# Joining chunk 0's inverse halves on TensorE, and moving raw-word transfers to SyncE's queue

## The chip, the cores and the metric

The kernel runs on one core of one Trainium2 chip. The time is device microseconds of one execution, as the median over several executions. A core has TensorE (PE, matrix multiply), VectorE (DVE), ScalarE (ACT), GpSimd (POOL) and SyncE (SP), each with its own instruction queue that runs in order; the queues wait for each other through semaphores. DMAs are issued here from SyncE's and GpSimd's queues. TensorE's clock is granted by a throttle, and the profile shows how much of full speed it was given.

## The reference

Two stages. A delta-rule recurrence over 768 steps for 4 batches and 8 heads, head dimension 48, and a feed-forward block on its output. Cut to what matters:

```python
k_n = k / (np.linalg.norm(k, axis=-1, keepdims=True) + 1e-06)
for t in range(S):                       # S = 768, state is (B, H, 48, 48)
    y[:, :, t] = einsum('bhd,bhde->bhe', q[:, :, t], state)
    v_old = einsum('bhde,bhd->bhe', state, k_n[:, :, t])
    state += beta[:, :, t, None, None] * outer(k_n[:, :, t], v[:, :, t] - v_old)
x = y.transpose(0, 2, 1, 3).reshape(3072, 384)
h = x @ w_in                             # (384, 2048)
out = (h / (1 + exp(-1.702 * h))) @ w_out  # (2048, 384)
```

The arithmetic is float32. The weights `moe_w_in` and `moe_w_out` arrive as 64-bit words; the kernel fetches them raw and turns them into float32 on VectorE.

## The kernel before, in words

The sequence is cut into 6 chunks of 128 steps. A *unit* is one chunk of one batch (8 heads), so there are 24 units; chunk 0 holds units 0 to 3. Inside a chunk the recurrence becomes a triangular solve: with G the Gram matrix of the normalized keys, the corrected values U satisfy (I + tril(beta G)) U = V. The 128 rows are cut into four blocks of 32 (`BS`). For each of the 128 diagonal blocks of a chunk (4 batches, 8 heads, 4 blocks: one per SBUF partition) VectorE builds the 32x32 inverse; the rest is block substitution on TensorE.

**The inverse** (`invert`, line 440) works on two tiles, `NT` (the blocks, row by row in the free dimension) and `YB` (their inverse, starting as the identity, stored with columns j before rows i). Sub-blocks of 8 are inverted row by row, pairs of 8 are joined to 16 (the `QS < HS` part), and the two halves of 16 are joined to 32: the lower left quarter is minus Y1 N10 Y0. Every product is a VectorE multiply into a scratch tile `P` followed by a reduce (`dots`). For chunk 0 the result is then transposed block by block into `YT` on the partitions of the time steps, and multiplied per unit by a scale (`zs[:, 5]`, beta over the squared norm) into `XB`, kept in `inverse[b]`.

**The hops** (`hops`, line 994, and `together`). A unit's solve is four times: U of block `blk` = XB times V (`solve`, psU, 8 matmuls of 32x32 on 48 columns), copied from PSUM by ScalarE (`solved`), then G times U for the blocks below (`below`, psR), subtracted from V by VectorE (`rest`). Two units alternate, so that eight hops (the loop at line 1033) solve units 0 and 1, and eight more units 2 and 3. Between hops the loop lays other work by hand: `ahead_of(preparing, 1)` (the keys of chunk 1: ScalarE squares, a VectorE sum, GpSimd's power, a VectorE scaling, then transposes, Gram matrices `G` and their way through DRAM into `NT`), `fill(n)` (n VectorE steps of the conversion of raw weight words), the scaling of V of units 2 and 3 (`values_scaled`, ScalarE), the causal masking of score tiles (`select`, GpSimd) and `warm(n)` (n throw-away bf16 matmuls of 128x256 on TensorE). After the hops `put_out` forms the outputs psY and the state; the first feed-forward matmuls (`ph`) follow.

**In front of the hops** TensorE transposes the keys (psT), forms the diagonal blocks (`diagonal`, psD) that VectorE scales into `D_` and turns into `NT`, the Gram matrices of chunk 0 (`gram`, psG, copied to G by ScalarE) and the scores of all four units (`scores`: psT of q, ScalarE's copy to QS, psQ, four ScalarE copies to M). PSUM is in three pools: `ps_big` (2 banks), `ps_moe` (2) and `ps_seq` (4). Chunk 0's psG uses `ps_moe` throughout, psT `ps_big`, psQ one pair in `ps_big` and one in `ps_seq`.

**The order** is that of the program: most instructions around the change are pinned (`Engine`, `pinned`; the helper is line 102, so the profile shows them all as L102). VectorE, ScalarE and GpSimd run them in that order, as does each DMA queue.

**Raw words.** `w_in` is fetched in four quarters by `fetch_in` (line 172). A quarter is three parts `j` of 128 rows, a part four DMAs: 48 and 16 rows for each half of the partitions. Quarters 0, 1 and 3 land in `w_out`'s tile (3 in the place of 0), quarter 2 in three spare tiles `homes` ("raw"). In quarters 0 to 2 the half for partitions from 64 on is issued by GpSimd's queue (`other_queue`), the other by SyncE's. A conversion step on VectorE waits for the words it reads. Each queue keeps eight DMAs under way: one more waits for the one eight places ahead.

## Time and profile before

| | |
|---|---|
| median of 3 executions | 773.48 us (773.38 to 776.35) |
| the profiled execution | 771.55 us, span 769.8 us |
| mean granted TensorE clock | 0.977 of full |
| TensorE busy | 743.6 us, 97% of the span |
| TensorE weight loads | 558.0 us, 72% |
| VectorE busy | 439.8 us, 57% |
| ScalarE busy | 240.1 us, 31% |
| GpSimd busy | 128.4 us, 17% |

The page gives busy time per engine over the whole span and in 40 slices of 19.2 us, each a digit in tenths. A busy TensorE counts the throw-away matmuls too. A timeline line reads: start, duration, engine, line, operation, output<-inputs, partitions x elements, count, and in brackets the idle time before it with what ended it. A float32 matmul appears as two records, so psU's 8 matmuls are x16. A table of stretches gives for each its length, then the busy time of PE, PEld, DVE, ACT and POOL with the number of instructions, the granted clock, the DMA engines' share and GB/s.

### The profile page before, as it was taken

The page shows a single profiled execution, that of the slowest core. Times are in us where ns is not written, and L with a number is a line of the kernel's source. Part 1 is how long each engine was busy: PE and PEld are TensorE (multiplying, and loading weights), DVE is VectorE, ACT ScalarE, POOL GpSimd, SP SyncE. Part 2 cuts the span into 40 slices and gives each one's busy share as a digit, 9 for nine tenths or more (in the row PEclk, how much of TensorE's full clock was granted, in tenths as well). Part 3 has the DMA queues.
Part 4 walks back from the last instruction along what each step waited for, and adds up shares of the span by engine and source line. Part 5 has one row for each costly group of instructions (what it writes and reads, how often), then busy time and mean ns, then how long its engine had stood idle before and what let it go on. Part 6 is the DMA issues. An engine that isn't in the chain of part 4 may idle for free.

```text
span 769.8 us, 19471 instructions
## 1 busy us (share of the span) xinstructions
PE 743.6 (97%) x8508; PEld 558.0 (72%) x8508; DVE 439.8 (57%) x896; ACT 240.1 (31%) x535; POOL 128.4 (17%) x133
## 2 busy tenths in 40 slices
PE   7888999888999999999999999999999999999997
PEld 6666788556687687687688678678678677686774
DVE  5999897996766566566566566565566521000000
ACT  4567523343233233133133133124123132121110
POOL 6133301100222122122131121220210000000000
PEclk8599999989999999999999999999999999999999
DMA  9965355543142142142142142142030020000000
GB/s 158 173 121 114 86 146 124 141 107 82 40 96 57 37 93 56 37 95 56 35 96 57 34 97 56 25 107 57 22 81 9 24 42 2 17 11 1 26 1 21
DMA packets 131637, 50.78 MB, mean 66 GB/s; under 512 B 106432, under 2 KB 127040, under 8 KB 131552
## 3 DMA queue, kind: packets, MB, share of 16 engines
q1 hardware_dynamic: 129152, 41.27, 24.9%
q0 software_dynamic: 2400, 8.26, 4.4%
q8 instruction: 67, 1.10, 0.6%
q14 instruction: 18, 0.15, 0.1%
HBM read 32.08 MB, written 16.25 MB: 63 GB/s over the span
## 4 chain that ended last, share of the span: by engine, by line
PE 83%; DVE 8%; SPq 4%; issue 1%; ACT 1%; DMA 1%; POOL 0%; DVEq 0%; ACTq 0%
PE ph L102 32%; PE po L102 30%; PE psY L102 6%; PE psU L102 5%; SPq L102 4%; PE psQ L102 3%; PE psR L102 3%; PE psG L102 2%; DVE w_out L102 2%; PE psT L102 2%; DVE tmp L102 2%; DVE P L102 1%; DVE V L102 1%; DVE w_in L102 1%; DMA w_out<-in_moe_w_in_dram 1%
## 5 line engine op out<-in xcount | busy, mean ns | idle before, releaser
L102 PE MATMUL po<-w_out,gT 128*128 128x384 f32 x768 | 263.4, 494 | 3.3 <-DVE w_out L102 3.3
L102 PE MATMUL ph<-xT,w_in 128*128 128x256 f32 x1152 | 261.2, 383 | 0.3
L102 PEld LDWEIGHTS ph<-xT,w_in 128*128 128x128 f32 x1152 | 214.8, 190 | 32.5 <-issue 1.7
L102 PEld LDWEIGHTS po<-w_out,gT 128*128 128x128 f32 x768 | 142.2, 191 | 96.3 <-DVE w_out L102 4.2
L102 DVE TENSOR_TENSOR V<-V,psR 128x384 f32<-128x384 f32 (+2 forms) x72 | 40.1, 557 | 191.6 <-PE psR L102 191.0
L102 ACT ACTIVATE gT<-ph 128x512 f32<-128x512 f32 x96 | 56.5, 596 | 150.8 <-PE ph L102 150.7
L102 DVE TENSOR_TENSOR P<-NT,YB 64x8 f32<-64x8 f32 (+26 forms) x178 | 85.2, 479 | 4.7
L102 ACT COPY US<-psU 32x384 f32<-32x384 f32 x92 | 43.2, 470 | 139.6 <-PE psR L102 75.5
L102 PEld LDWEIGHTS psU<-V,XB 32*32 32x32 f32 x1536 | 58.3, 104 | 35.8 <-issue 25.6
L102 DVE TENSOR_REDUCE YB<-P 64x4 f32<-64x8 f32 (+27 forms) x178 | 77.2, 434 | 6.3 <-DVE P L102 0.2
L102 PE MATMUL psU<-V,XB 32*32 32x48 f32 x1536 | 69.5, 203 | 4.0 <-DVE V L102 3.9
L102 PE MATMUL psR<-US,G 32*32 32x48 f32 x2576 | 62.9, 204 | 1.0 <-issue 0.5
L624 POOL TENSOR_SCALAR_AFFINE_SELECT M<-M 128x1024 f32<-128x1024 f32 x20 | 25.1, 1253 | 220.9 <-DVE M L102 160.1
L102 PEld LDWEIGHTS psR<-US,G 32*32 32x32 f32 x2576 | 53.4, 104 | 2.0 <-issue 1.0
L102 PE MATMUL psQ<-QS,kT 48*128 48x176 f32 (+1 forms) x384 | 39.1, 350 | 5.4 <-ACT QS L102 5.4
L102 PEld LDWEIGHTS psQ<-QS,kT 48*128 48x128 f32 x384 | 32.1, 215 | 9.0 <-ACT QS L102 7.2
L102 DVE TENSOR_TENSOR P<-NT 64x256 f32<-64x256 f32 (+7 forms) x44 | 36.3, 825 | 0.3
L102 DVE TENSOR_REDUCE NT<-P 64x64 f32<-64x1024 f32 (+7 forms) x44 | 35.4, 803 | 1.5
L102 PE MATMUL psG<-kT 48*128 48x128 f32 x384 | 32.1, 304 | 1.9 <-ACT G L102 1.2
L102 ACT COPY o<-po 128x384 f32<-128x384 f32 x24 | 11.5, 479 | 71.5 <-issue 41.0
L87 POOL DMA_DIRECT2D KN<-in_k_dram x13 | 12.4, 953 | 116.1 <-PE psY L102 107.0
L102 ACT COPY M<-psQ 128x256 f32<-128x256 f32 x68 | 22.9, 377 | 24.8 <-DVE V L102 17.5
(102 smaller groups left out, 609.7 us busy)
## 6 DMA issues: line engine op xcount, KB each, us to landing
Nd<-G SPq DMA_DIRECT2D x16, 512.0 KB, 3.5
QP<-in_q_dram SPq DMA_DIRECT2D x24, 192.0 KB, 3.9
V<-in_v_dram SPq DMA_DIRECT2D x24, 192.0 KB, 3.3
out_dram<-o SPq DMA_DIRECT2D x24, 192.0 KB, 2.0
KN<-in_k_dram POOLq DMA_DIRECT2D x14, 192.0 KB, 3.8
NT<-Nd SPq DMA_DIRECT2D x20, 128.0 KB, 2.6
Yd<-YS SPq DMA_DIRECT2D x20, 128.0 KB, 2.5
XB<-Yd SPq DMA_DIRECT2D x20, 128.0 KB, 3.0
```

What stands on the lines that cost most here:

```text
L87: dma(out=dst[n % len(dst)][:, :, 0:D], in_=src[b, :, c * C : (c + 1) * C, :].rearrange("h p d -> p h d"),)
L102: return lambda *a, **kw: tc.keep_in_program_order(op(*a, **kw))
L624: (pool if self.n < B else nc.gpsimd).affine_select(out=self.M, in_=self.M, compare_op=ALU.is_gt, fill=0.0, base=0, pattern=[[0, H], [1, 1 ...
```

## The change

Chunk 0's inverse stops at the halves of 16. VectorE transposes the upper half's columns of Y into `YT`, the lower half into `Yb` (in `NT`, its other columns zeroed by GpSimd) and the lower columns into `YT`. `joined` then joins the halves of one unit on TensorE in two steps, one yield each: psZ (32 matmuls from `D_`, the 32x32 blocks, and Y1 transposed), copied over `D_` by ScalarE, and psC (32 matmuls with Yb), which VectorE subtracts from `YT` before it forms XB. Unit 0 is joined before the hops, unit 1's psC follows the first hop's solve, and units 2 and 3 are joined in hops 1 to 4. `YT` lies in the third spare tile of quarter 2.

Around it: psG of units 1 and 3 uses `ps_big`; the scores of units 0 to 2 are formed two transposes ahead with bursts of 4 warm matmuls between, those of unit 3 in hops 2 and 3; the burst before the joins is 12 in place of 26 in front of the hops (`NY`), and in the first eight hops 5 in each but hop 3, which has none, where it was 11 in the first three and 5 in the others. GpSimd's queue keeps its half of quarter 0; quarters 1 and 2 are issued by SyncE alone, the last part of each after the joins that free its place. q of unit 3, k of unit 6 and 7 (`seventh`), the values of units 2 and 3, q of unit 4 and the later betas change places in SyncE's queue.

```diff
-    NW, NY, NU = 14, 26, 11
+    NW, NS_, NY, NU = 14, 4, 12, 11
-    def fetch_in(i, other=None):
+    def fetch_in(i, other=None, js=range(KC)):
-        for j in range(KC):
+        for j in js:
 def gram(n):
-        pool_, tag = (ps_moe, "moe") if c == 0 else (ps_big, "big")
+        pool_, tag = (ps_moe, "moe") if c == 0 and b % 2 == 0 else (ps_big, "big")
 def invert(c, b0=0, nb=B):
+        if c == 0:
+            by_d = Yb.rearrange("p d j -> p j d")
+            vec.transpose(YT.rearrange("p d i -> p i d")[:, HS:], Y.rearrange("p j i -> p i j")[:, HS:])
+            pool.memset(Yb[:, :, HS:], 0.0)
+            vec.transpose(by_d[:, 0:HS], Y[:, 0:HS])
+            vec.transpose(YT.rearrange("p d i -> p i d")[:, 0:HS], Y.rearrange("p j i -> p i j")[:, 0:HS])
+            yield 0.0
+            return
-        if c == 0:
-            T = wk.tile([128, BS, BS], F32, tag="P", name="YT")
-            vec.transpose(T.rearrange("p d i -> p i d"), Y.rearrange("p j i -> p i j"))
-            for b in range(B):
-                XB = wk.tile([128, H, BS], F32, tag="XB", name="XB", bufs=4)
-                tt(XB, T[:, b * H : (b + 1) * H], zs[:, 5, b].broadcast_to([128, H, BS]), op=ALU.mult)
-                inverse[b] = XB
-                yield 0.0
-            return
+    def joined(bs):
+        HS, n = BS // 2, len(bs)
+        d = slice(bs[0] * H, (bs[-1] + 1) * H)
+        blocks = [slice(blk * BS, (blk + 1) * BS) for blk in range(NB)]
+        Z = D_[:, bs[0] : bs[-1] + 1, :, 0:HS]
+        ps = ps_moe.tile([128, n, H, HS], F32, tag="moe", name="psZ")
+        for i, b in enumerate(bs):
+            for h in range(H):
+                for r in blocks:
+                    pe.matmul(ps[r, i, h, :], lhsT=D_[r, b, h, :], rhs=YT[r, b * H + h, HS:], start=True, stop=True)
+        act.copy(Z, ps)
+        yield
+        ps = ps_moe.tile([128, n, H, HS], F32, tag="moe", name="psC")
+        for i, b in enumerate(bs):
+            for h in range(H):
+                for r in blocks:
+                    u = slice(r.start, r.start + HS)
+                    pe.matmul(ps[r, i, h, :], lhsT=Yb[u, b * H + h, :], rhs=Z[u, i, h, :], start=True, stop=True)
+        vec.tensor_tensor(YT[:, d, HS:], YT[:, d, HS:], ps.rearrange("p n h i -> p (n h) i"), op=ALU.subtract)
+        for b in bs:
+            XB = wk.tile([128, H, BS], F32, tag="XB", name="XB", bufs=4)
+            vec.tensor_tensor(XB, YT[:, b * H : (b + 1) * H], zs[:, 5, b].broadcast_to([128, H, BS]), op=ALU.mult)
+            inverse[b] = XB
+        yield
 # the loads in front
-    for b in range(B):
+    for b in range(B - 1):
         load(b, ((QP, q),), sync)
-    for n in range(B, len(KN)):
+    for n in range(B, len(KN) - 1):
         load(n, ((KN, k),), sync)
-    fetch_in(1, other_queue)
-    for b in range(HB, B):
-        load_values(b, sync)
+    load(B - 1, ((QP, q),), sync)
+    fetch_in(1, js=range(KC - 1))
-    fetch_in(2, other_queue)
-    for blk in range(NB):
-        sync(out=bI[blk::NB, 1:], in_=betas[:, 1:, blk, :])
# scores, inverse and joins
-    seventh = blocks[:, 0 : H * D].rearrange("p (h d) -> p h d", h=H)
-    load(len(KN), (([seventh], k),), sync)
-    inverting = invert(0)
-    for n in range(B):
-        for _ in pair[n].scored:
-            pass
-    run(inverting)
+    YT = homes[KC - 1].bitcast(F32).rearrange("p (d i) -> p d i", i=BS)
+    Yb = NT
+    scored = [s.scored for s in pair]
+    next(scored[0])
+    next(scored[1])
+    warm(NS_)
+    run(scored[0])
+    warm(NS_)
+    next(scored[2])
+    run(scored[1])
+    warm(NS_)
+    run(scored[2])
-    for s in pair[:HB]:
-        values_scaled(s, range(H))
-    pool.tensor_copy(landed, YB[:, 0, BS - 1 : BS])
-    for s in pair[:HB]:
-        s.select()
-    pool.tensor_copy(landed, inverse[B - 1][:, 0, 0:1])
+    values_scaled(pair[0], range(H))
+    run(invert(0))
     warm(NY)
+    joins = [joined(bs) for bs in ([0], [1], [2], [3])]
+    next(joins[0])
+    next(joins[1])
+    next(joins[0])
+    values_scaled(pair[1], range(H))
+    seventh = blocks[:, 0 : H * D].rearrange("p (h d) -> p h d", h=H)
+    def after_joins():
+        next(joins[1])
+        load(len(KN), (([seventh], k),), sync)
+        fetch_in(1, js=[KC - 1])
+        load(len(KN) - 1, ((KN, k),), sync)
+        for b in range(HB, B):
+            load_values(b, sync)
+            pair[b].V = loaded.pop(b)
+        load(B, ((QP, q),), sync)
+        fetch_in(2, js=range(KC - 1))
+        for blk in range(NB):
+            sync(out=bI[blk::NB, 1:], in_=betas[:, 1:, blk, :])
+        pool.tensor_copy(landed, inverse[1][:, 0, 0:1])
+        for s in pair[:HB]:
+            s.select()
-    load(B, ((QP, q),), sync)
# the first eight hops
     for i in range(2 * NB):
         together(*next(path))
+        if i == 0:
+            after_joins()
+        elif i < 5:
+            next(joins[2 + (i - 1) % 2])
+        if i == 4:
+            fetch_in(2, js=[KC - 1])
+        if i == 2:
+            next(scored[3])
+        elif i == 3:
+            run(scored[3])
         ahead_of(preparing, 1)
         fill(1 + i % 2 if i else 5)
...
-        warm(NU if i < 3 else NU // 2)
+        warm(NU // 2 if i != 3 else 0)
         ahead_of(preparing, 1)
```

More of the change, by code (lines that the diff above doesn't have):

```diff
@@ L132, in warm @@
     def warm(n):
+        if n == 0:
+            return
         ps = ps_moe.tile([128, 256], F32, tag="moe", name="ps_warm")
@@ L500, in invert @@
                 yield 0.0
+        if c == 0:
[5 more added lines that the diff above has]
+            yield 0.0
+            return
         X1 = N[:, 0:HS, HS:]
@@ L527, in invert @@
             yield 0.0
-        if c == 0:
-            T = wk.tile([128, BS, BS], F32, tag="P", name="YT")
-            vec.transpose(T.rearrange("p d i -> p i d"), Y.rearrange("p j i -> p i j"))
-            for b in range(B):
-                XB = wk.tile([128, H, BS], F32, tag="XB", name="XB", bufs=4)
-                tt(
-                    XB, T[:, b * H : (b + 1) * H],
-                    zs[:, 5, b].broadcast_to([128, H, BS]), op=ALU.mult,
-                )
-                inverse[b] = XB
-                yield 0.0
-            return
         YS = wk.tile([128, BS, BS], F32, tag="P", name="YS")[part]
@@ L556, in invert @@
         yield 0.0
+    def joined(bs):
[7 more added lines that the diff above has]
+                for r in blocks:
+                    pe.matmul(
+                        ps[r, i, h, :], lhsT=D_[r, b, h, :], rhs=YT[r, b * H + h, HS:],
+                        start=True, stop=True,
+                    )
+        act.copy(Z, ps)
[5 more added lines that the diff above has]
+                    u = slice(r.start, r.start + HS)
+                    pe.matmul(
+                        ps[r, i, h, :], lhsT=Yb[u, b * H + h, :], rhs=Z[u, i, h, :],
+                        start=True, stop=True,
+                    )
+        vec.tensor_tensor(
+            YT[:, d, HS:], YT[:, d, HS:], ps.rearrange("p n h i -> p (n h) i"), op=ALU.subtract
+        )
+        for b in bs:
+            XB = wk.tile([128, H, BS], F32, tag="XB", name="XB", bufs=4)
+            vec.tensor_tensor(
+                XB, YT[:, b * H : (b + 1) * H], zs[:, 5, b].broadcast_to([128, H, BS]), op=ALU.mult
+            )
+            inverse[b] = XB
+        yield
     def bank(name, shape=(128, H, D)):
@@ L575, in __init__ @@
             self.qp = QP[n % len(QP)]
-            self.n, self.V = n, loaded.pop(n)
+            self.n, self.V = n, loaded.pop(n, None)
             self.US = late_U if n == B - 1 else US[n % len(US)]
@@ L941 @@
         load_values(b, sync)
-    for n in range(B, len(KN)):
+    for n in range(B, len(KN) - 1):
         load(n, ((KN, k),), sync)
-    fetch_in(1, other_queue)
-    for b in range(HB, B):
-        load_values(b, sync)
+    load(B - 1, ((QP, q),), sync)
+    fetch_in(1, js=range(KC - 1))
     blocks = spare("blocks")
     D_ = blocks.rearrange("p (b h k) -> p b h k", b=B, k=BS)
-    fetch_in(2, other_queue)
-    for blk in range(NB):
-        sync(out=bI[blk::NB, 1:], in_=betas[:, 1:, blk, :])
+    quarter(2)
     room = spare("U")
```

## The prediction

> **What bounds the kernel now.** I read the slices of the profile's page first: TensorE is at nine tenths from the fourth slice on, but in the first four (77 us) VectorE is the fuller engine, and in slices two and three the granted TensorE clock reads 5 and 9. So the head decides differently from the rest, and the change is in the head.
>
> ```profile
> PE   7888999888999999999999999999999999999997
> DVE  5999897996766566566566566565566521000000
> PEclk8599999989999999999999999999999999999999
> ```
>
> Then VectorE's timeline of the head. From 13.5 to 50.3 us it has no idle piece; these lines frame what the change takes out.
>
> ```profile
> 25.59 0.69 DVE L102 TENSOR_REDUCE YB<-P 128x64 f32<-128x512 f32 x1
> 26.31 0.39 DVE L102 COPY NT<-YB 128x256 f32<-128x256 f32 x1
> ...
> 39.55 2.00 DVE L102 STREAM_TRANSPOSE YT<-YB 128x1024 f32<-128x1024 f32 x1
> 41.58 1.63 DVE L102 TENSOR_TENSOR XB<-YT,U 128x256 f32<-128x256 f32 x4
> 43.13 0.68 DVE L102 TENSOR_SCALAR w_in<-w_out 128x768 int32<-128x768 int32 x1
> ```
>
> TensorE's timeline shows who waits: scores end at 37.8, 26 warm matmuls fill the time to 42.57, and the first solve (psU) runs as soon as the inverse is there.
>
> ```profile
> 14.34 2.56 PE L102 MATMUL psG<-kT 48*128 48x128 f32 x16 [0.68 <-ACT G L102]
> ...
> 35.72 2.08 PE L102 MATMUL psQ<-QS,kT 48*128 48x128 f32 x16 [0.69 <-ACT QS L102]
> 37.73 4.84 PE L102 MATMUL ps_warm<-ident 128*128 128x256 bf16 x26
> 42.50 0.86 PE L102 MATMUL psU<-V,XB 32*32 32x48 f32 x16
> ```
>
> Last the busy time in stretches of 3.41 us, cut where the granted clock changes (14.2 down, 41.5 up, 164.4 down). Columns: span, PE, PEld, DVE, ACT, POOL, clock, DMA share, GB/s.
>
> ```profile
> 10.79:14.20 3.41, 1.85 (x81) 1.61 (x80) 3.00 (x14) 0.51 (x2) 1.28 (x4) 1.00 1.04 209
> 14.20:17.60 3.40, 2.99 (x18) 2.69 (x18) 3.16 (x7) 1.65 (x4) 2.08 (x5) 0.50 1.19 165
> 38.10:41.50 3.40, 3.40 (x18) 2.43 (x16) 3.33 (x3) 3.40 (x16) 1.85 (x3) 0.50 1.18 171
> 51.80:55.20 3.40, 2.03 (x58) 1.62 (x57) 3.31 (x6) 1.01 (x2) 1.59 (x1) 1.00 0.02 5
> 160.80:164.20 3.40, 2.01 (x36) 1.11 (x34) 3.30 (x9) 1.56 (x3) 0.00 (x0) 1.00 0.92 237
> ```
>
> The clock falls after stretches with TensorE 54% and 59% busy, holds after 60%, and comes back only after a full one, not after 92%. The chain of waits runs through SyncE's queue until a landing of raw words at 45.58, but VectorE's instruction before that one ends at 45.66; I take VectorE as the bound to 43, and keep the transfers as a rival. From 42.5 to 61.2 VectorE is busy 18.02 of 18.70 us, and from about 82 us TensorE runs without gaps to 130, so a shift of the hops should reach the end undiminished.
>
> **The change, part by part.**
>
> *Off VectorE.* Unit by unit nothing changes until 26.28 (25.59 + 0.69). Out go the copy, eight pairs of multiply and reduce, the transpose and four XB multiplies: 26.31 to 43.21, 16.9 us. In come three half transposes at half of 2.00, 1.0 each, and per unit a subtract of 128 elements (I take 0.28, between 0.19 for 128x32 and 0.42 for 128x256) and its XB (1.63 / 4 = 0.41). The first half transpose ends at 27.3, the second 28.3, the third 29.3.
>
> *Joins on TensorE.* psZ and psC are 32 matmuls of 32x32 on 16 columns each, 64 records. Nearest rows: psD, 64 records, 0.74 to 0.89 us; and psU with psR, 80 records in 1.47 us (44.60 to 46.07), so 1.18 for 64. I take 0.8, since psD too fills separate array tiles in turn; the end 1.18 costs 0.38 more on each of the four in front of the first hops, 1.5; the lower end, by fewer columns, 0.5, gives 1.2 back.
>
> Against this stands the Trainium skill, "TensorE: Matmul & The Clock Gate", section "Wait — 56ns, not 53.3ns?", which states that the start-to-start of matmuls never drops below about 25 ns. That would make 64 records 1.6 us, an estimate from that page, and the gain about 3.2 us smaller.
>
> The psD row has 11.9 ns a record, so the row decides.
>
> *The path to the first hop.* psZ of unit 0 27.35 to 28.15, of unit 1 to 28.95; ScalarE's copy of Z 0.27 (the 128x128 copy is 0.26) hides beside the second psZ; psC of unit 0 to 29.75; 0.15 to VectorE; subtract and XB to 30.6; psU at 30.75 in place of 42.50: 11.75 earlier. Then a new wait: psC of unit 1 stands behind that psU (0.86) on TensorE, so it ends at 32.4, and unit 1's subtract and XB at 33.25. VectorE idles for it, and behind it queue the five conversion steps and V of the second hop, 3.9 us later as before (43.13 to 47.04): 37.15 against 47.04, 9.9 earlier. Units 2 and 3 add 0.7 each to a VectorE that has 0.68 us free in 18.7: 8.5. I take off 0.5 for waits of these two subtracts and for unit 3's scores, whose QS and M copies (0.6 + 1.3 us) now lie among the US copies on ScalarE. TensorE there does 4 joins and the scores, about 3.2 + 1.8 us, less 25 warm matmuls at 0.125, 3.1; it has 3.3 free. **Sum: 8.0 us earlier**, between 9.2 and 6.0 by the bounds above and up to 0.5 us more on each late join.
>
> *Scores and gram in front.* They must end before 27.3, or psZ waits. At full clock: four psG at 1.16 from 12.49, ScalarE's copies (1.08 each) end at 18.2, the first psT starts with the third bank, 17.65; three psT at 0.66, three psQ at 1.16 (as psG), 24 warm at 0.125 and two bank waits of 0.35 are 9.2 us: 26.85, 0.45 early. The clock decides that. psG of unit 1 now takes the other pool and follows unit 0's without the 0.68 wait: the stretch to 14.2 is then busy from 11.81 on, 2.39 of 3.41, 70%, over the 60% that held. But if the stretches lie otherwise in a run, one can hold most of the 1.9 us gap before 11.81 and fall at 45%. Then the four psG at half clock (2.3 each) leave no gap, because the copies are shorter, and a full stretch should bring the clock back by 19.3: psZ 2 us late.
>
> The same page's section "What's actually happening" says that the clock falls after at least one idle window and is released by one busy window. By it the clock would not have fallen at 14.2, where no window was idle, and the sum would be 8.0 with no chance kept for rivals 1 and 3.
>
> The rows say otherwise: a part-idle stretch was enough, and 92% did not release it. They decide, and by them those rivals stay.
>
> *Transfers.* Twelve raw pieces of quarters 1 and 2 leave POOL's queue (0.51 us each) for SyncE's (0.42 each, 5 us of issue in all), eight of them and k before the joins. POOL's share is then gone after quarter 0, about 16 us, and SyncE alone moved 171 to 198 GB/s from 34 to 46. By that rate q lands by 19, v by 21.5, k by 24 and two thirds of quarter 1 by 31. The k of unit 7 (seventh) now waits for psC of unit 1 (32.4), and behind it on SyncE queue quarter 1's last third, a k, two v, a q, quarter 2 and the betas, then quarter 3 and the Nd copies. Quarter 1 is needed for its conversion at 53.45, now 44.6: 0.2 + 0.5 MB after 32.5 lands by 37 at that rate, by 41.4 with a 5.0 us landing behind 4 us of queue. Quarter 3 ends near 58; xT's copies follow at 64.4 instead of 71.45 and land by 70, needed at 74 (81.98 less 8). So nothing, with 3 to 4 us of cover in both places.
>
> *Others at nothing.* POOL's memset of Yb (half of 0.96) ends before psC; its two selects (2.14) now wait for XB of unit 1, 33.3 to 35.5, ahead of the power for the first ssq at 38. Unit 0's V scaling fits on ScalarE before Z; unit 1's (1.86) is done before psU's copy.
>
> **Forecast.** The profiled execution took 771.55, of which the span is 769.84; it becomes 763.5. It lies 1.9 below the median, so against 773.48 I say **765.5**; likeliest case's own range 764 to 767.5.
>
> **Rivals.**
> 1. *A clock that falls for a while*, before the joins (2 us, above) or in the hops: after the second hop TensorE waits from 36.55 to 38.0 for V, 42% of a stretch, with a warm burst of 5 where there were 11. At half clock that stage is TensorE's, is full, and recovers in two stretches; 6.8 us at some 35% excess, 2.4. Gives 767.5 to 769.5. For it: the fall at 59%; against: 60% held at 51.8.
> 2. *Transfers set the pace.* If SyncE alone reached only the 120 GB/s of the third slice of the profile's page, the 4.75 MB after 32.5 would last 39.6 us, to 72, and xT (13 us behind as in before, less overlap) would land near 82: ph again at its old time, 773. For it: the chain's landing at 45.58, and 20 transfers behind one wait. Against: 183 GB/s from 34 to 46.
> 3. *Slower: the clock stays at half until the joins.* The gram ends at 21.3 (12.49, 1.16, three of 2.56), psT from 21.9, three psT at 1.11, three psQ at 2.08, 24 warm at 0.22, two waits of 0.69: psZ at 38. That is 10.7 behind 27.3, and three joins at double length add 2.4: 5.1 slower than before, 778.5. It decides from psZ later than 35.3, where the 8 us are spent. For it: before, 82 to 92% busy kept the half clock for 27 us. Against: the waits that made those gaps go, and warm bursts stand between.
>
> **How the numbers follow.** Forecast 0.50; rival 1 0.25; between the two and no gain (rival 2, or a clock that returns in mid-scores, psZ 3 to 7 late: 769 to 773) 0.15; rival 3 0.10. Half a per cent, what a measurement tells from no change, is 3.9 us: faster below 769.6, slower above 777.3. Forecast and rival 1 are faster, so 0.75; the third case 0.15 is about the same; rival 3 0.10 slower. The range leaves out rival 3, the top of the third case and a gain above 9.8: 763.7 to 772.5.
>
> **What would show it.** Right: first psU near 31, the clock at 1.0 from about 8 to 60, V of the second hop near 37, the first ph near 74, VectorE idle only at the two joins. Wrong: psZ waiting for TensorE's own warm matmuls or psQ beyond 28; conversions waiting for a landing; ph waiting on xT; a clock of 0.5 past 20.

## The result, and the profile after

The changed kernel takes **778.38 us** in the median of 13 executions (776.45 to 780.82) against 773.47 for the kernel before on the same chip: a ratio of 1.0057, with a 95% interval of 1.0039 to 1.0075. The ratios are those on record with their intervals, and differ a little from the quotient of two medians (1.0063 here); the kernel before alone spreads from 771.1 to 776.5. The change is slower by a little over half a per cent, where 765.5 was forecast. The profiled execution took 779.64 us, its span 777.8 (before: 771.55 and 769.8), so the sum to be explained against the profiled forecast of 763.5 is 16 us, and against the medians 13.

The slices of the profile's page, and the line of the queue that carries TensorE's instructions (columns: packets, MB, share of 16 engines):

```profile
PE   6789999887999999999999999999999999999998
DVE  6576898895866566666666665666665531000000
PEclk9755999998999999999999999999999999999999
...
q8 instruction: 71, 1.16, 0.6%
```

The same line of the kernel before:

```profile
q8 instruction: 67, 1.10, 0.6%
```

VectorE is less full in the second slice, which is what the change was to bring. But the clock reads 5 in slices three and four, where before it read 5 in the second alone. Four more packets of instructions are fetched; a packet has 16,384 bytes. Both profiles count TensorE's records, 8,508 before and 8,995 after, and 8,995 / 71 is 127 to a packet.

TensorE's timeline of the head says where the time goes first:

```profile
11.96 4.35 PE L102 MATMUL psG<-kT 48*128 48x128 f32 x63
20.48 0.33 PE L102 MATMUL psG<-kT 48*128 48x128 f32 x1 [4.17 <-issue]
...
30.66 1.28 PE L102 MATMUL psZ<-raw,blocks 32*32 32x16 f32 x128
32.13 0.52 PE L102 MATMUL psC<-blocks,NT 16*32 16x16 f32 x41 [0.18 <-issue]
34.37 0.52 PE L102 MATMUL psC<-blocks,NT 16*32 16x16 f32 x23 [1.72 <-issue]
35.75 1.40 PE L102 MATMUL psU<-V,XB 32*32 32x48 f32 x15 [0.86 <-DVE XB L102]
...
46.10 0.84 PE L102 MATMUL psZ<-raw,blocks 32*32 32x16 f32 x44
48.57 0.50 PE L102 MATMUL psZ<-raw,blocks 32*32 32x16 f32 x18 [1.63 <-issue]
```

The reader is to see three breaks *inside* runs of equal matmuls: after 63 of 64 psG, after 41 of 64 psC, after 46 of 64 psZ (two of them stand in lines of their own). No operand is late there; the profile calls the wait "issue". Counted from the first matmul, the breaks of the head come after records 221, 349, 603, 858 and 986: distances of 128, 254, 255 and 128 (some records can be missing from a trace, and it counts no other instructions). The first of these breaks was there before the change, inside a run of equal psD and after the same 221 records (as in every profile here), as the line of the kernel before shows:

```profile
11.81 0.76 PE L102 MATMUL psD<-kT 48*32 48x32 f32 x65 [1.90 <-issue]
```

A matmul record has a weight load beside it, so 128 records are 256 instructions, one packet of 16,384 bytes. Around the psC break the trace has such a packet from 31.94 to 33.17, and TensorE goes on at 34.37. The block edge before that one fell behind 41 records of psZ, at about 31.06. From edge to resumption are thus 3.3 us, and the joins had used up the 128 records between the two edges in 1.6.

VectorE's timeline shows what follows (the four V are those of the second to the fifth hop):

```profile
34.95 0.29 DVE L102 TENSOR_TENSOR raw<-raw,psC 128x128 f32<-128x128 f32 x1 [5.99 <-PE psC L102]
...
43.69 0.54 DVE L102 TENSOR_TENSOR V<-V,psR 128x384 f32<-128x384 f32 x1
46.45 0.56 DVE L102 TENSOR_TENSOR V<-V,psR 128x384 f32<-128x384 f32 x1
52.69 0.56 DVE L102 TENSOR_TENSOR V<-V,psR 64x384 f32<-64x384 f32 x1 [3.69 <-PE psR L102]
56.94 0.56 DVE L102 TENSOR_TENSOR V<-V,psR 64x384 f32<-64x384 f32 x1 [0.78 <-PE psR L102]
```

The second and the fourth in the kernel before:

```profile
47.04 0.54 DVE L102 TENSOR_TENSOR V<-V,psR 128x384 f32<-128x384 f32 x1
52.39 0.56 DVE L102 TENSOR_TENSOR V<-V,psR 64x384 f32<-64x384 f32 x1
```

VectorE's last transpose ends at 28.95 (forecast 29.3), and then it waits 5.99 us for the join. The first psU is at 35.75: 6.75 earlier than before, 5.0 later than forecast. V of the second hop is 3.35 earlier than before, V of the fourth (which the expectation of later calls the third) 0.3 later: the hops give back what was won, and the first ph comes at 88.49, where it was 81.98. That is 6.5 of the 8.0 us by which the profiled span grew; the rest lies behind it.

Nearly all of the hops run at half clock: it falls at 34.2 and is back only at 75.2 (before: half from 14.2 to 41.5, in front of the hops). Busy times in stretches of 3.40 us, columns as for the kernel before:

```profile
30.60:34.00 3.40, 1.87 (x171) 1.64 (x169) 0.00 (x0) 3.40 (x16) 0.00 (x0) 1.00 0.03 6
44.20:47.60 3.40, 2.65 (x128) 2.13 (x128) 3.17 (x8) 0.66 (x3) 2.32 (x1) 0.50 0.85 175
51.00:54.40 3.40, 3.40 (x123) 3.25 (x124) 1.43 (x4) 0.63 (x2) 0.00 (x0) 0.50 0.41 82
61.20:64.60 3.40, 3.40 (x30) 2.58 (x31) 2.93 (x4) 1.83 (x5) 2.10 (x2) 0.50 0.93 193
```

The stretch with the psC break has TensorE 55% busy, and the clock falls at its end. From 51 on TensorE shows as fully busy at half clock, VectorE is not (1.43 of 3.40): at half clock TensorE sets the pace of the hops.

### The profile page after: what moved, and what is told of

It reads as the page before. It is cut to its first block, busy times and chain, and to the rows that moved or that the text cites. A ratio compares the mean times of both kernels' runs of the same rounds, so it can differ in the third digit from the quotient of the medians.

```text
span 777.8 us, 20438 instructions
## 1 busy us (share of the span) xinstructions
PE 750.3 (96%) x8995; PEld 565.9 (73%) x8995; DVE 429.3 (55%) x885; ACT 240.5 (31%) x539; POOL 120.8 (16%) x121
## 4 chain that ended last, share of the span: by engine, by line
PE 90%; DVE 6%; issue 2%; ACT 1%; DMA 0%; POOL 0%; POOLq 0%; ACTq 0%
PE ph L102 31%; PE po L102 30%; PE psU L102 6%; PE psY L102 6%; PE psQ L102 4%; PE psG L102 4%; PE psT L102 3%; PE psR L102 3%; PE ps_warm L102 2%; DVE w_out L102 2%; DVE tmp L102 1%; DVE P L102 1%; DVE YB L102 1%; PE psC L102 0%; DVE V L102 0%
## 5 line engine op out<-in xcount | busy, mean ns | idle before, releaser
L102 PEld LDWEIGHTS psU<-V,XB 32*32 32x32 f32 x1536 | 63.5, 111 | 33.8 <-issue 27.1
L102 DVE TENSOR_TENSOR P<-NT,YB 64x18 f32<-64x18 f32 (+23 forms) x174 | 80.8, 464 | 4.7
L102 DVE TENSOR_REDUCE YB<-P 64x6 f32<-64x18 f32 (+23 forms) x174 | 73.9, 425 | 6.0
L102 PE MATMUL psU<-V,XB 32*32 32x48 f32 x1536 | 75.2, 211 | 0.9 <-DVE XB L102 0.9
L102 PE MATMUL psR<-US,G 32*32 32x48 f32 x2576 | 67.6, 211 | 0.0
L102 PEld LDWEIGHTS psR<-US,G 32*32 32x32 f32 x2576 | 57.9, 109 | 0.7 <-ACT w_out L102 0.3
L102 PE MATMUL psQ<-QS,kT 48*128 48x176 f32 (+1 forms) x384 | 35.8, 325 | 2.9 <-ACT QS L102 2.9
L102 PEld LDWEIGHTS psQ<-QS,kT 48*128 48x128 f32 x384 | 29.1, 194 | 5.9 <-ACT QS L102 3.8
L102 DVE TENSOR_TENSOR P<-NT 64x256 f32<-64x256 f32 (+7 forms) x40 | 33.0, 825 | 0.3
L102 DVE TENSOR_REDUCE NT<-P 64x64 f32<-64x1024 f32 (+7 forms) x40 | 32.1, 801 | 1.4
```

Of the source, the lines that this page charges most:

```text
L102: return lambda *a, **kw: tc.keep_in_program_order(op(*a, **kw))
```

## The experiments

The theories, as the expectations name them. **F**: TensorE waits for the fetch of its own instructions, because the joins are 256 fp32 matmuls, 512 records, four blocks of 128. **C**: the chain of the joins leaves TensorE idle, the clock falls, and the number of matmuls does not matter. **S**: SyncE's queue alone brings the raw words too late. Later ones: **H**, the half clock through the hops is what costs, and **J**, the joins in the hops make it; **W**, TensorE's own work in the hops, at whatever clock; **L**, a hop with the 64 records of a join loses its clock through the fetch; **P**, a place behind the hops where scores were moved to. Each run is compared with runs of the kernel before on its chip, whose medians were 773.25 to 774.17.

### few: the joins in an eighth of the matmuls

```diff
             for h in range(H):        # psZ; psC likewise
-                for r in blocks:
-                    pe.matmul(ps[r, i, h, :], lhsT=D_[r, b, h, :], rhs=YT[r, b * H + h, HS:], ...)
+            for r in blocks:
+                pe.matmul(ps[r, i, :, :], lhsT=D_[r, b, 0, :], rhs=YT[r, b * H : (b + 1) * H, HS:], ...)
```

> The changed kernel with 4 matmuls in each psZ and each psC in place of 32: each works on 128 columns and uses head 0's block for all eight heads, so the joined inverse is not the reference's; all waits, copies and subtracts stay. Theory F (TensorE's instructions arrive in blocks of 256, 128 matmul records, and the joins' 64 records a step eat them faster than they arrive): the idle stretches put down to issue after 30 us (1.72, 0.79, 1.63 us) go, the one of 4.17 us in the gram at 16.3 stays since it lies ahead of the joins; first psU at 32.5 to 33.5 in place of 35.75, the clock does not fall at 34.2, and the whole takes 767 to 771. Theory C (the clock falls because the chain psZ, copy, psC, subtract, XB leaves TensorE idle whatever the number of matmuls): the clock still falls at about 34, time 775 to 778. Theory S (transfers on SyncE's queue alone are late): nothing changes, 777 to 780.

Measured: **766.44 us** (764.56 to 766.64), ratio 0.9914 (0.9896 to 0.9931). TensorE's timeline:

```profile
30.61 0.64 PE L102 MATMUL psZ<-raw,blocks 32*32 32x128 f32 x16
32.08 0.42 PE L102 MATMUL psC<-blocks,NT 16*32 16x128 f32 x8 [0.83 <-issue]
33.36 0.82 PE L102 MATMUL psU<-V,XB 32*32 32x48 f32 x15 [0.86 <-DVE XB L102]
```

The break inside psC is gone (the 0.83 stands ahead of its first matmul, where Z is copied), psU is 2.4 earlier, the clock is half from 34.8 to 45.0 only, and V of the hops follow each other in 2.7 to 3.5 us. With the same columns and the same dependences, and with other blocks as weights, the time is 0.9 above the forecast 765.5. The number of matmuls is worth 11.9 us. The clock did fall at 34.8, which was C's mark and not F's, but it was back after 10 us, and the time is 8.6 us below C's range (and 0.6 below F's 767 to 771), so C falls. What the 11.9 us consist of is not settled by this run alone: the joins' own TensorE time between 30 and 60 us falls as well, from 8.8 to 4.0 us, in part by the clock.

### stuffed: the kernel before, with 256 idle records

```diff
+    ps = ps_moe.tile([128, H, BS // 2], F32, tag="moe", name="psF")
+    for _ in range(4):                 # x H x NB: 128 matmuls of 32x32 on 16 columns
+        ...
+                pe.matmul(ps[r, h, :], lhsT=D_[r, B - 1, h, :], rhs=D_[r, B - 1, h, 0 : BS // 2], ...)
     warm(NY)
```

> The kernel before with 128 float32 matmuls of 32x32 on 16 columns (256 records, two blocks of instructions) put in ahead of the 26 warm matmuls; their result is not used. By their own time at half clock, 1.1 us for 64 records in the changed kernel, they take 4.4 us, so with no fetch cost the first psU comes at 47 and the whole is 4 to 5 us slower. Theory F: one or two idle stretches put down to issue of 1 to 4 us each, 128 records apart, on top: first psU at 48.5 to 53, the whole 6 to 10 us slower. Theories C and S: no idle stretch in the stream, 4 to 5 us slower.

```profile
36.89 2.53 PE L102 MATMUL psF<-blocks 32*32 32x16 f32 x173
43.18 1.35 PE L102 MATMUL psF<-blocks 32*32 32x16 f32 x83 [3.76 <-issue]
44.47 4.08 PE L102 MATMUL ps_warm<-ident 128*128 128x256 bf16 x26
48.48 0.86 PE L102 MATMUL psU<-V,XB 32*32 32x48 f32 x16
```

Measured 777.40 us (776.09 to 779.48), ratio 1.0064 (1.0041 to 1.0087); psU at 48.48, where F had 48.5 to 53. The time is 4.2 us above the median before, which is C's and S's range and not F's 6 to 10; F's mark is the break in the stream, which C and S excluded. Small matmuls without any dependence stop in mid-run for 3.76 us in a kernel without joins. A packet lands at 41.69, TensorE goes on at 43.18.

### quiet and sync_alone: the transfers

```diff
# quiet, on the changed kernel: quarter 1 wholly after unit 1's join
-    fetch_in(1, js=range(KC - 1))
-        fetch_in(1, js=[KC - 1])
+        fetch_in(1)
# sync_alone, on the kernel before
-    fetch_in(1, other_queue)
+    fetch_in(1)
-    fetch_in(2, other_queue)
+    fetch_in(2)
```

> The changed kernel with the first two thirds of quarter 1 fetched behind the join of unit 1, not ahead of it, so that the DMA engines have less to do from 22 to 33 us. Theory F with a fetch that waits behind other transfers: the instruction packets after 24 us start sooner after the block before them is used up, and the wait in psC shrinks from 1.72 to under 0.8; the gram's 4.17 stays. First psU near 34.5; but the conversion of quarter 1, wanted at 54.6, is served later. Time 774 to 778. Theory C: no change at the joins, 778. Theory S: SyncE's backlog after the joins grows by 1 MB, some 5 us, and the time with it: 781 to 784.

> The kernel before with quarters 1 and 2 of the raw words issued by SyncE's queue alone, in their old places, and nothing else. Theories F and C: no part of the loss, within 0.3% of the kernel before; under F the gram might even wait less, since q and k meet fewer raw words. Theory S: slower by 3 us or more.

Measured: quiet 779.71 us (777.02 to 781.07), 1.0085 (1.0056 to 1.0113); sync_alone 774.30 (770.13 to 777.86), 1.0005 (0.9978 to 1.0031). The half of the change that moves raw words costs nothing that can be measured, and S falls. For quiet the expectation was wrong in a useful way: the breaks in the joins stayed or grew (2.00 in psC, 2.45 in psZ). Little else was moved in the psC stretch anyway (6 GB/s above), so it is not transfers that make the 3.3 us. The break in psG is 2.79 where it was 4.17, but that is not the edit's doing: the transfers that it moves are issued from 22.2 us on in the changed kernel, behind that break, and psG goes on no earlier (20.72 against 20.48). The clock was half from 13.7 to 17.1 in this execution, so the work ahead of the break took longer. No run here changes the traffic around psG.

### few_front and few_late: which joins

The edit of few with a condition: for psZ of units 0 and 1 and psC of unit 0 alone, or for the other joins, those in the hops, alone.

> The changed kernel with the joins in front of the hops alone in few matmuls: psZ of units 0 and 1 and psC of unit 0 are 4 matmuls on 128 columns each where they were 32 on 16 (head 0's block for all heads, so the output is not the reference's); the joins in the hops keep their 32. TensorE's instruction fetch (F) expects the 1.72 us stall in psC of unit 0 to go, and psU near 33.5 where it was 35.75. From there two theories part. H (the half clock from 34.2 to 75.2 makes the rest of the loss, and a front without the stall lets the clock come back as in 'few', at 45): half no later than 55, time 767 to 772. J (the joins in the hops, with their 0.79 and 1.63 us stalls, make it): the clock stays at half beyond 65 and the time falls by the 2 us of the front alone, 775.5 to 777.

> The changed kernel with the joins in the hops alone in few matmuls: psC of unit 1 and psZ and psC of units 2 and 3 (output not the reference's); those in front of the hops keep their 32. psU stays near 35.75 by F. H (the fall at 34.2 is the front's doing and TensorE has even less to fill a stretch with): the clock stays at half beyond 65 and the time is 774 to 778. J (joins in the hops): the two stalls of 0.79 and 1.63 us and some 1.1 us a join at half clock go, the clock is back by 55, and the time is 768 to 772.

Measured: few_front 773.98 us (772.60 to 776.32), 1.0000 (0.9978 to 1.0021), half clock from 36.9 to 71.0; few_late 769.78 (768.49 to 773.96), 0.9946 (0.9919 to 0.9973), half from 34.0 to 47.6, and psU at 35.67 as expected. Against the changed kernel the joins in front are worth 4.4 us and those in the hops 8.6, together 13.0 where few gained 11.9. J had the marks of both (clock past 65 in the one, back by 55 in the other), though few_front lies below its 775.5 to 777, with psU at 34.71 where near 33.5 was expected. H in its first form, that the front decides about the clock in the hops, falls.

### wide: longer warm matmuls in the hops

```diff
-        warm(NU // 2 if i != 3 else 0)
+        warm(NU // 2 if i != 3 else 0, 2)      # 512 columns each
```

> The changed kernel with the warm matmuls of the first eight hops on 512 columns where they had 256, the same number of matmuls and so the same blocks of 128 records. F expects every stall and psU (35.75) as in the changed kernel. H: with some 1.1 us more of TensorE a hop at half clock a stretch is filled, the clock is back between 42 and 55, and the time is 769 to 775. J, or a half clock that is only the mark of a TensorE that is the bound anyway: the added work comes on top, 778 to 784.

Measured 776.07 us (772.68 to 782.71), 1.0030 (0.9998 to 1.0061). In the profiled execution, which took 780.48, the clock was also down from 20.7 to 34.4 and psU at 38.09; it came back at 54.8, fell at 58.3 and came back at 68.5. H had 769 to 775, J 778 to 784; with times 10 us apart this decides nothing between the two.

### bd: the same products in 16 records a join

```diff
+    def spread(dst, src):              # GpSimd: 32x32 blocks onto the diagonals of 128x128
+        for blk in range(NB):
+            r = slice(blk * BS, (blk + 1) * BS)
+            pool.tensor_copy(dst[r, :, r], src[r])
 ...
             for h in range(H):         # psZ; psC of units 1 to 3 likewise, from BY and Z
-                for r in blocks:
-                    pe.matmul(ps[r, i, h, :], lhsT=D_[r, b, h, :], ...)
+                pe.matmul(ps[:, i, h, :], lhsT=BD[b % 2][:, h, :], rhs=YT[:, b * H + h, HS:], ...)
```

> The changed kernel with the same products in fewer matmuls: GpSimd spreads the 32x32 blocks of a unit onto the diagonals of 128x128 tiles (in the part of w_in that is filled last), and psZ of all units and psC of units 1 to 3 are 8 matmuls of 128x128 on 16 columns, 16 records, where they were 32 and 64; psC of unit 0 stays. 176 records of joins in the place of 512, so the kernel has 336 fewer records, 2.6 blocks. A join of 16 records costs between 0.2 us (at psZ's 10 ns a record) and 1.3 us (at the 83 ns a record of psT). F: no stall in the joins, psU between 33 and 35, clock back by 55, and a time of 766 to 772, near 'few' (766.44). If the stalls were not the number of matmuls but something else in that stretch (the many transfers behind the joins), psU stays at 35.5 or later and the time at 776 or more.

Measured **790.31 us** (788.64 to 791.95), 1.0193 (1.0164 to 1.0223), where F had 766 to 772, with half clock from 33.9 to 88.5: a miss. No join is interrupted any more, but a join of 16 records of 128x128 weights takes 3.60 us at half clock, where the 64 small ones take 1.10; the two psZ in front take 4.69 together where they took 1.28. My bound of 0.2 to 1.3 us was taken from rows with 128 columns to move, where they move; here the weight loads alone were busy for 4.61 of those 4.69 us. Fewer instructions are no gain where each gets longer than the fetch it saves.

### aligned, later and both: the same matmuls, elsewhere

Aligned has 41 records fewer in front of the joins, later moves the joins of units 2 and 3 by two hops, both is the two together:

```diff
# aligned
-    warm(NW)
+    warm(NW // 2, 2)
     # likewise warm(NS_ // 2, 2) twice and warm(NY // 2, 2);
     # next(scored[2]) and run(scored[2]) go to hops 5 and 6 (both: 6 and 7),
     # its masking to hop 7, that of unit 3 to hop 5
# later
-        elif i < 5:
-            next(joins[2 + (i - 1) % 2])
-        if i == 4:
+        elif 3 <= i < 7:
+            next(joins[2 + (i - 3) % 2])
+        if i == 6:
             fetch_in(2, js=[KC - 1])
     # the scores of unit 3 in hops 1 and 2 in the place of 2 and 3
```

> The changed kernel with 41 records fewer in front of the joins (nothing left out): the warm matmuls there are half as many on 512 columns, and the scores of unit 2 move to hops 5 and 6. By the counted records the block edge that fell behind 41 of psC's 64 records then falls behind the first psU. F: no stall in psZ or psC, psU between 31.5 and 33.5 in place of 35.75, a stall of at most 1 us in psC of unit 1 instead; the joins in the hops are as before, so the gain is at most the 4.4 us of 'few_front', less up to 1.8 us of scores: 773 to 777. Rival (the stall belongs to psC, whatever was counted before it): psU at 34 or later and 777 to 780.

> The changed kernel with the joins of units 2 and 3 two hops later, in hops 3 to 6 in the place of 1 to 4, and the scores of unit 3 in hops 1 and 2 (nothing left out; the last part of quarter 2 is fetched two hops later too). In hops 1 and 2 psU and psR are 80 records, in 3 and 4 48, in 5 and 6 32, so the joins leave 101 to 105 and about 120 records in a hop where there were 165. F (a hop cannot be shorter than the fetch of its records, 3.3 us for 128): psU stays at 35.75, the 1.63 us stall in psZ goes, V of the third hop comes at 49 where it was 52.69, and the time is 769 to 775, between 'few_late' (769.78) and the changed kernel. Rival (the half clock alone, with TensorE's work the same wherever the joins lie): half until 70 or later, 776 to 780.

> 'later' and 'aligned' together, nothing left out. F: psU between 31.5 and 33.5, no stall over 1 us from there to the end of the eight hops, the clock back by 50, and 765 to 771, near 'few' (766.44) and below the kernel before. Rival (half clock alone): half until 65 or later, 774 to 779.

Aligned: 774.48 us (773.61 to 776.28), 1.0004 (0.9984 to 1.0024). Its TensorE timeline:

```profile
26.86 1.27 PE L102 MATMUL psZ<-raw,blocks 32*32 32x16 f32 x128 [0.94 <-DVE raw L102]
28.01 0.72 PE L102 MATMUL psC<-blocks,NT 16*32 16x16 f32 x64
29.59 1.48 PE L102 MATMUL psU<-V,XB 32*32 32x48 f32 x16 [0.86 <-DVE XB L102]
30.88 0.28 PE L102 MATMUL psC<-blocks,NT 16*32 16x16 f32 x2
32.57 1.05 PE L102 MATMUL psC<-blocks,NT 16*32 16x16 f32 x62 [1.41 <-issue]
```

This is the sharpest reading of the study. 41 records were taken away, and the break moved from record 41 of unit 0's psC to record 2 of unit 1's, which is 41 records later (23 psC, 16 psU, 2 psC). The breaks in the hops that follow, 0.36 and 0.70 us, stand after 858 and 986 records, as in the changed kernel, but now inside psR. The wait belongs to the count, not to the operation. psU comes at 29.59, earlier than even the forecast's 30.75. Of these 6.2 us, 3.8 are psZ's earlier start (26.86, with unit 2's scores gone from in front and no long break in psG) and 2.4 the way from psZ to psU. The expected marks were a psU of 31.5 to 33.5, a break of at most 1 us and 773 to 777; the time met them, and the break was 1.41.

But later took 776.81 us (774.12 to 779.33), 1.0041 (1.0017 to 1.0065), where F had 769 to 775, and both 774.44 (771.17 to 776.25), 0.9996 (0.9967 to 1.0025), where F had 765 to 771. Both times lie in the range of the rival, the half clock alone (776 to 780 and 774 to 779). F's marks in later came all the same: the 1.63 us break in psZ is gone (one of 0.85 is left, two hops later), and V of the fourth hop is at 47.64. Both has no "issue" wait at all from the first psU to the end of the hops, and still:

```profile
30.60:34.00 3.40, 3.40 (x101) 2.77 (x99) 1.35 (x4) 0.89 (x2) 0.64 (x2) 0.50 0.25 53
51.00:54.40 3.40, 3.40 (x94) 3.08 (x91) 2.59 (x5) 0.57 (x2) 0.80 (x1) 0.50 0.81 189
61.20:64.60 3.40, 3.40 (x34) 3.28 (x34) 3.33 (x5) 2.76 (x10) 2.27 (x1) 0.50 0.50 87
```

The clock was half from 28.0 to 69.0, with TensorE shown as busy for 39.8 of these 41.0 us. So the fetch is not the whole of it: once the clock is down, TensorE's work in the hops keeps the pace low by itself.

### after_burst and both_burst: bring the clock back

```diff
-        warm(NU // 2 if i != 3 else 0)
+        if i == 1:
+            warm(16, 2)
+        else:
+            warm(NU // 2 if i != 3 else 0)
```

> The changed kernel with 16 warm matmuls on 512 columns in hop 1 in the place of 5 on 256: at half clock 16 x 0.43 = 6.9 us without a gap, longer than two stretches of 3.41, so that one whole stretch lies in it. Theory H (the half clock through the hops is what costs; the stalls only bring it on): the clock is back by 48 where it was 75.2; the burst itself delays hop 2 by 4 to 5.6 us, the hops after it go from 4.25 to some 3.3 us, so the first ph comes before its 88.49 and the time is 770 to 776. Rival W (TensorE's own work and its stalls in the hops cost, at whatever clock): the burst comes on top, 781 to 785, or the clock falls again at once and stays at half.

> 'both' (no stall left after the first psU, yet half clock from 28.0 to 69.0 and 774.44) with the same burst of 16 in hop 1. H: clock back by 46, hops 2 to 7 at 3 us in place of some 4.2, 4 to 5.6 us given for the burst: 767 to 773. W: 778 to 781.

Measured: after_burst 779.41 us (777.54 to 784.04), 1.0074 (1.0049 to 1.0100); both_burst 776.03 (772.08 to 779.20), 1.0019 (0.9996 to 1.0041). The burst did what it was to do to the clock (back at 47.1 and 43.9), and the time was not won: the clock fell again at 53.9 and 50.7, and both times lie between the ranges of H and W. The line and stretches of both_burst:

```profile
44.20:47.60 3.40, 3.40 (x106) 2.40 (x104) 1.24 (x4) 1.17 (x4) 0.00 (x0) 1.00 1.07 255
47.60:51.00 3.40, 2.22 (x125) 1.80 (x125) 3.13 (x6) 2.02 (x6) 0.92 (x1) 0.96 0.49 106
51.00:54.40 3.40, 3.40 (x116) 3.18 (x114) 2.39 (x6) 1.58 (x4) 0.83 (x1) 0.50 0.32 93
```

At full clock a hop with a join runs out of instructions again (1.05 us behind 50, 1.75 at 54.41 in after_burst), the stretch is 65% busy, and the clock goes. Neither H nor W as stated: in these two profiles the hops are caught between the fetch at full clock and TensorE's own work at half.

### both_few_late, both_nowarm, after_nowarm

```diff
# both_nowarm, after_nowarm: on both, and on the changed kernel
-        warm(NU // 2 if i != 3 else 0)
+        warm(NU // 2 if i == 0 else 0)
```

> 'both' with the joins in the hops (psC of unit 1, psZ and psC of units 2 and 3) as 4 matmuls on 128 columns where they were 32 (output not the reference's), so a hop has at most 101 records. If the loss left in 'both' is the 64 records that a join adds to a hop (L: at full clock such a hop waits for its instructions, and the waiting costs it the clock; at half clock it is TensorE's), the clock is back by 52 and stays, and the time is 763 to 769. If the half clock after the joins in front holds whatever the hops carry (H alone): half beyond 62, 771 to 775.

> 'both' without the warm matmuls in hops 1 to 7 (nothing left out). L and H: at half clock TensorE sets the pace in hops 2 to 7, VectorE waits for psR three times (1.49, 1.50, 1.57 us), and each burst of 5 costs 1.25 us there, so the hops gain 4 to 5 us: 768 to 772 as long as the clock comes back near 69 as in 'both'. Rival (the warm matmuls bring the clock back): half beyond 75, 774 to 780.

> The changed kernel without the warm matmuls in hops 1 to 7 (nothing left out). L and H: in hops 3 to 7 TensorE sets the pace at half clock (VectorE waits 0.78 to 1.61 us for psR in four hops), so 3 to 4 us go: 773 to 776. Rival (the warm matmuls bring the clock back): half beyond 80, 778 to 784.

Measured: both_few_late 772.21 us (768.74 to 775.84), 0.9970 (0.9948 to 0.9993); both_nowarm 772.01 (770.31 to 772.85), 0.9967 (0.9947 to 0.9987); after_nowarm 776.20 (774.31 to 782.91), 1.0031 (1.0003 to 1.0060). Without the joins' records the clock was back at 49.8, as L had it, but fell again from 60.0 to 66.8, and the time missed L's 763 to 769 and lies in H's 771 to 775. The cut that was worth 8.6 us from the changed kernel to few_late is worth 2.2 us here. Without warm matmuls the time falls by some 2 us in both kernels (2.4 and 2.2, with intervals that overlap; 5.0 from early to early_nowarm below), and the clock comes back no later (67.2 and 71.6, where it was 69.0 and 75.2): at half clock these matmuls are a cost and do not release it.

### early and early_nowarm

On both, with the scores of unit 2 in hops 0 and 1 in the place of 6 and 7; early_nowarm also without warm matmuls in hops 1 to 7.

> 'both' with the scores of unit 2 in hops 0 and 1 in the place of 6 and 7 (psT, psQ; nothing left out). In 'both_few_late' psG waited 3.00 us for the M copies of these scores ahead of psY, and VectorE 5.36 us for xT. If this placement is what 'both' and its kind lost behind the hops (P), the wait goes, the stage from the last V of the hops to the first V of the next eight shrinks from some 18 us towards the 12.8 of 'few', and the time is 768 to 772. If that wait was only the half clock's, 773 to 776.

> 'early' without the warm matmuls in hops 1 to 7 (nothing left out). P, with TensorE at half clock setting the hops' pace: the 2.4 us of 'both_nowarm' on top, 765 to 770, below the kernel before by 0.5 to 1%. Rival (the half clock's wait): 770 to 773.

Measured: early 773.73 us (769.98 to 776.18), 0.9997 (0.9975 to 1.0020); early_nowarm **768.77** (767.18 to 769.71), 0.9923 (0.9899 to 0.9947). Early alone shows no gain and lies in the rival's 773 to 776, so P is not confirmed; VectorE still waited 3.40 us for xT behind its hops. Together with the warm matmuls out, the wait is 0.79 and the first ph is at 76.30. TensorE's and VectorE's timelines of early_nowarm:

```profile
29.74 1.48 PE L102 MATMUL psU<-V,XB 32*32 32x48 f32 x16 [0.84 <-DVE XB L102]
31.74 1.04 PE L102 MATMUL psC<-blocks,NT 16*32 16x16 f32 x62 [0.44 <-issue]
```

```profile
38.39 0.54 DVE L102 TENSOR_TENSOR V<-V,psR 128x384 f32<-128x384 f32 x1
42.19 0.56 DVE L102 TENSOR_TENSOR V<-V,psR 128x384 f32<-128x384 f32 x1 [1.07 <-PE psR L102]
45.60 0.56 DVE L102 TENSOR_TENSOR V<-V,psR 64x384 f32<-64x384 f32 x1 [1.08 <-PE psR L102]
```

One break of 0.44 us is left, V of the fourth hop is 7 us earlier than in the changed kernel, and the clock is half from 28.3 to 62.5. This version leaves nothing out and beats both kernels: by 0.77% the one before (interval 0.53 to 1.01%; by the medians 4.6 us), and by 9.6 us the changed one. It had four executions.

### The runs side by side

| run | median us | ratio to before | first psU | half clock in the hops | first ph |
|---|---|---|---|---|---|
| before | 773.47 | 1 | 42.50 | none | 81.98 |
| changed | 778.38 | 1.0057 | 35.75 | 34.2-75.2 | 88.49 |
| few | 766.44 | 0.9914 | 33.36 | 34.8-45.0 | 75.60 |
| few_front | 773.98 | 1.0000 | 34.71 | 36.9-71.0 | 84.54 |
| few_late | 769.78 | 0.9946 | 35.67 | 34.0-47.6, 61.3-64.7 | 78.38 |
| aligned | 774.48 | 1.0004 | 29.59 | 28.8-66.4 | 83.71 |
| both | 774.44 | 0.9996 | 30.08 | 28.0-69.0 | 83.25 |
| both_burst | 776.03 | 1.0019 | 32.69 | 33.7-43.9, 50.7-74.6 | 88.05 |
| both_nowarm | 772.01 | 0.9967 | 29.79 | 29.6-67.2 | 81.21 |
| early_nowarm | 768.77 | 0.9923 | 29.74 | 28.3-62.5 | 76.30 |

Times are medians; the last three columns are of the one profiled execution, which lies up to 3.2 us off its median. In all nine profiles with joins in this table the span is 688.9 to 689.4 us longer than the first ph's start: among them, what the head wins or loses arrives at the end whole. It is 687.9 in the kernel before, and 686.6 in early and bd, which the table leaves out.

## Why the prediction was wrong

The forecast's direction and size both failed, at two steps: **the working has no term for the supply of TensorE's instructions**, and **it lets a clock that has fallen come back after one or two full stretches**. The terms one by one:

- *What bounds the kernel, and that a shift of the hops reaches the end undiminished*: right within some 1.5 us, by the last sentences above.
- *Off VectorE*: right. The third transpose ends at 28.95 (forecast 29.3), the subtract takes 0.29 (0.28), XB 0.43 (0.41).
- *Joins on TensorE, 0.8 us each*: the busy time was even less, 1.28 for two psZ at full clock, 10 ns a record, so the trace's psD row was the right one against the 25 ns of the Trainium skill, "TensorE: Matmul & The Clock Gate", section "Wait — 56ns, not 53.3ns?". What the step lacked is that 64 records are also half a block of instructions. 192 records of joins stand in front of the first psU, and the trace shows 3.3 us for the supply of 128. The profile of before could have warned: it lists 67 packets on the instruction queue for 8,508 records, and the 1.9 us gap before 11.81, which the prediction names, is such a break. A bound from it was within reach of the working and was not asked for.
- *Scores and gram in front, 26.85*: they ended at 30.66. The 4.17 us break behind 63 of 64 psG makes up the difference, and with it the clock, which held until 20.6, went for one stretch.
- *The path to the first hop, 30.75*: 35.75, of which 3.3 are psZ's start (30.66 against 27.35) and 1.72 the psC break. In six of the seven variants with 41 records fewer in front psU came at 29.59 to 30.18, with psZ starting at 26.84 to 27.46.
- *Units 2 and 3: TensorE has 3.3 us free in the hops*: wrong. With psU and psR, 80 records, a join, 64, four of a transpose and 5 warm matmuls, the third hop has 153 records (not the 165 of an expectation), 3.9 us of supply at 3.3 for 128, where the hops of few took 2.7 to 3.5. It is in these hops that few_late won its 8.6 us. (The 25 warm matmuls that the step takes off are 23 in the hops and 2 in front.)
- *Rival 1, a clock that falls for a while, 2.4 us*: this is what happened, only that it lasted 41 us and not two stretches. The step that failed in it is that a full stretch brings the clock back. In the changed kernel six stretches shown as full, from 51.0 to 71.4, did not.
- *Rival 3, slower, 778.5*: its number was hit by luck, by another way. It needed psZ later than 35.3; psZ started at 30.66, and the clock fell behind the joins and not in front of them.
- *Transfers*: right; sync_alone, with the transfers in their old places, is at 1.0005, and in the new places neither VectorE nor TensorE waits for a landing in the hops.

The Trainium skill, "Runtime: NRT & Kernel Launch", section "Instruction fetch mechanics", states that an engine's instructions come in blocks of 16 KiB, 256 instructions, over a DMA queue of its own, the next block fetched while the present one runs. The 16,384-byte packets and the breaks at every 128 records agree with that. The same section calls the cost mostly hidden; here it was 1.72 us in the joins and 4.17 in front, since 128 records of small matmuls last 1.6 us. Of the deeper store that it gives TensorE, eight blocks, no run here shows anything: the packet of the psC break starts 0.9 us after the edge before it.

What stays open: which measure of TensorE's work releases the clock. One full stretch did it in few_late (44.2 to 47.6), though one from 37.4 to 40.8 had not, and six did not in the changed kernel; matmuls' ends are modelled in the profile, so small ones may fill less than it shows. The 8.6 us of the late joins are therefore not split here between waits for instructions and half clock. The bursts show that a stretch with such a wait loses the clock; both, which has no such wait and is still 8.9 us above the forecast, shows that the half clock does not need them to last.

## What to carry to other kernels

Count the records of a stretch and not their busy time alone: here 128 records were a block, and in the joins 3.3 us passed from one edge until TensorE went on behind the next, where the records themselves last 1.6; a change that trades VectorE work for hundreds of tiny matmuls has that price, and the page's instruction queue shows how many blocks it adds. A wait marked "issue" in the middle of equal matmuls, at distances of 128, is this and no dependence, and taking records out in front of it moves it. Throw-away matmuls that bring the clock back in one place (the bursts) look like a plain cost in another, where the clock is down anyway and TensorE sets the pace (2 to 5 us in three pairs of runs).

## What was not expected of the hardware

- TensorE ran dry on its instruction supply with its DMA queue at 0.6% of the engines' time: in the head of the changed kernel packets take 0.9 to 1.5 us, and TensorE resumes 1.2 to 1.8 us after one has landed.
- In the front of the changed kernel the same takes longer: from the edge at about 9.6 to the resumption at 20.48 (packet from 17.39), some 11 us. The DMA engines moved 181 GB/s from 9.6 to 17.4 and 6 around the psC break; that this is the reason fits and is not shown.
- At full clock a stretch 70% busy lost the clock in few_late (2.38 of 3.40, 57.8 to 61.2), where 60% held in the kernel before (51.8 to 55.2).
- A matmul of 128x128 weights on 16 columns costs 146 ns a record (4.69 us for 32, partly at half clock), one of 32x32 on 16 columns 10.
